# Moving the low-half subtraction of gathered token blocks to GpSimd, with x kept multiplied by 8

## The chip, the cores and the metric

One Trainium2 chip, of which the kernel uses one core. The metric is device time in microseconds (us) of one execution. The engines are named as in the profile: PE is TensorE (PEld its weight loads), DVE is VectorE, ACT is ScalarE, POOL is GpSimd, SP is SyncE, which here only issues DMAs. All engines run their own instructions in order, and wait for each other by semaphores.

## The reference

Two stages. First an attention over q, k, v of shape (8, 8, 576, 64): the sum of a coarse attention (tokens averaged in fours, its result repeated four times) and a local one (each token attends to those less than 4 away). Its output, laid out as x of 4608 tokens by 512, goes into a mixture of 8 experts with a fixed capacity of 576 tokens each:

```
logits = x @ w_gate                       # (4608, 8)
order = np.argsort(-logits.flatten())     # best (token, expert) pair first
for idx in order:                         # a token goes to the first expert that still has room
    tok, e = idx // E, idx % E
    if assigned[tok] >= 0 or counts[e] >= cap: continue
    assigned[tok] = e; counts[e] += 1
for e in range(E):
    mask = assigned == e
    out[mask] = np.maximum(x[mask] @ w1[e], 0) @ w2[e]     # 512 -> 1024 -> 512
```

## The kernel before

The first 280 us of the profile are the attention (class Attention). It works through 36 blocks of 128 tokens. For each block `norm` (L399) divides the local result by its softmax sum, `log_a` adds the coarse result, `store` writes the block of x to DRAM (x_dram), and `log_t` and `log_m` compute the gate's logits: x is transposed on PE, scaled by XS = 32 into a float16 high half and a float16 low half (L498, L499), and multiplied by the gate weights. The coarse result is normalized by the same `norm`, called in `down_v`. The order of this stage is written out by hand and does not depend on the engines' times.

Then the experts. The greedy assignment is solved one expert at a time: `Routing.phase` finds which expert fills next, and at what threshold, by counting. Compares on DVE (L709), counting matmuls on PE (L743, L750, L757, in PSUM tiles pR) and small DVE steps (L747, L752, L759, L729, L735) alternate in a long chain; at its end a one-hot product on PE (L992) and `idx` on DVE (L1001) give the 576 token numbers. Each phase needs the one before it. Below, E0 to E7 are the experts in the order in which they are found and run, and the phase of a later expert runs beside the matrix work of an earlier one.

For one expert:

- `weights` loads w1 and w2 (4 loads of 1 MB, from SP's queue, L1032); `split` turns each into a float16 high half on ACT (wh, L1048) and low half on DVE (wl, L1050).
- `gather` fetches the tokens in five blocks c = 0 to 4 (four of 128 tokens, one of 64) by indirect DMA issued on GpSimd (xg, L1065). `piece_dma(c)` then makes the high half of the block, scaled by XM = 8, on ACT (xs, L1084), the low half on DVE (L1085), and has SP transpose both by DMA into xt (L1086). There are XSB = 2 buffers xs, so the third block waits until the first transpose is done. Only E0 uses `piece` instead, which transposes on PE (L1074 to L1078).
- `mlp` computes the first product in eight passes f (pH, L1101; in each pass the first 256 tokens, then the other 320, with three matmuls for high by high, high by low and low by high), with ht split into halves on ACT and DVE (L1114, L1117); then the second product in five blocks c (pX, L1130, 24 matmuls each, 120 in all, in two PSUM buffers), which ACT scales into y (L1135) and GpSimd scatters to the output by indirect DMA (out_dram, L1138).

The order here is not written by hand: a scheduler that estimates the instructions' times lists them per engine. `in2` places the gathered blocks of the next expert: blocks 0 and 1 are to be issued after y of block c = 0, blocks 2 and 3 after c = 1, block 4 after c = 2 (table GET; for E1 this is a lower bound only, since its gather comes later). The subtraction and the copy are marked as high priority. A DVE instruction that waits therefore holds every DVE instruction behind it, those of the routing too, and PE's counting matmuls stand in PE's queue between those of pH and pX, so that PE waits with them.

Of the kernel before, what the change touches and what calls it, by code (L numbers as in the profile page):

```python
# [11 lines left out]
AF = mybir.ActivationFunctionType  # L12
OP = mybir.AluOpType
# [16 lines left out]
NTOK = B * S  # L30
NT = NTOK // 128
E, F = 8, 1024
XS = 32.0
GSN = ('k2',)
SH1 = 0.416
EARLY = 1
# [53 lines left out]
class Attention:  # L90
# [273 lines left out]
    def down_v(self, b, g):  # L364
        nc = self.nc
        vd = self.vd[b % 2]
        pt = self.ptd[b]
        o = self.ps.tile([128, 512], F32, name="g", bufs=8)

        nc.tensor.matmul(o[:, :260], pt[:, 9], vd[:, 1, 4 * g:4 * g + 4].rearrange("p h d -> p (h d)"),  # L370
                         start=True, stop=False, skip_group_check=True)
        for j in range(4):
            nc.tensor.matmul(o[:, 65 * j:65 * j + 65], pt[:, 4 * g + j], vd[:, 0, 4 * g + j],  # L373
                             start=False, stop=True, skip_group_check=True)
        x = self.wk.tile([128, 5, D], F32, name="xu", bufs=2)
        if g:

            for i in range(2):
                for c in range(2):
                    for hp in range(HP):  # L380
                        r = slice(32 * hp, 32 * hp + 32)
                        nc.tensor.matmul(o[r, 260 + 65 * i:325 + 65 * i], pt[:, 10 if c else 8, r], vd[:, c, 2 * hp + i],
                                         start=c == 0, stop=c == 1, skip_group_check=True, tile_position=(0, 32 * hp))
        def end():
            r = self.norm(o, x[:, :4], 4 + g, 4.0)
            up = self.up_dram[b * G:b * G + 128, 256 * g:256 * g + 256]
            nc.sync.dma_start(up, x[:, :4].rearrange("p h d -> p (h d)"))
            if g:
                own = self.wk.tile([128, 2], F32, name="own")
                nc.vector.tensor_tensor(own, r[:, 4:].to_broadcast([128, 2]), self.half, op=OP.mult)  # L390
                y = x[:, 4]
                nc.vector.tensor_scalar(y, o[:, 260:324], own[:, :1], None, op0=OP.mult)
                nc.vector.scalar_tensor_tensor(y, o[:, 325:389], own[:, 1:], y, op0=OP.mult, op1=OP.add)
                nc.sync.dma_start(bass.AP(tensor=up.tensor, offset=up.offset - 256 * g + 128 * HD,
                                          ap=[[D, H], [HD, 16], [1, D]]), y)

        self.after(FN, end, ("v", b, g))

    def norm(self, o, dst, m, n):  # L399
# [67 lines left out]
    def loc_v(self, u, g):  # L467
        nc = self.nc
        if g == 0:
            self.x[u] = self.wk.tile([128, HD], F32, name="x", bufs=XB)  # L470
        x = self.x[u]
        o = self.ps.tile([128, 512], F32, name="g", bufs=8)
        pt = self.ptw[u % NPT]
        for h in range(4):
            for i in range(2):
                nc.tensor.matmul(o[64 * i:64 * i + 64, 65 * h:65 * h + 65],  # L476
                                 pt[:, 2 * g + i, h].rearrange("p b q -> p (b q)"),
                                 self.vw[u % 4][:, i, 4 * g + h], start=True, stop=True)
        self.norm(o, x[:, 256 * g:256 * g + 256].rearrange("p (h d) -> p h d", h=4), 4, 1.0)

    def log_a(self, u):
        nc = self.nc
# [6 lines left out]
    def log_t(self, u):  # L489
# [3 lines left out]
        for c in range(4):  # L493
# [3 lines left out]
        hi = xt[:, 0].rearrange("p c t -> p (c t)")  # L497
        nc.scalar.activation(hi, pf, AF.Copy, scale=XS)  # L498
        self.after(FT, lambda: nc.vector.scalar_tensor_tensor(xt[:, 1].rearrange("p c t -> p (c t)"), pf, XS, hi,  # L499
                                                              op0=OP.mult, op1=OP.subtract), ("x", u))  # L500
# [116 lines left out]
            self.nc.tensor.matmul(p, w, w[:, None].to_broadcast([128, 4, 128]), start=True, stop=True)  # L617
# [1 line left out]

W1S, W2S, XM = 64.0, 64.0, 8.0  # L620
LOP = 512
CAP = NTOK // E
LV = ((64, 1024), (32, 32), (32, 1))
SW = 16
WHOLE = ((0, NT),)
HALF = {16: ((0, NT),), 32: ((0, 20), (20, NT)), 64: ((0, 20), (20, NT)), 128: ((0, 12), (12, 24), (24, NT))}
XSB = 2
LOE = "vector"
RACT = True
EH = ((0, 18), (18, NT))  # L630
SPP = ("xh", "xl")
# [373 lines left out]
class Experts:  # L1005
# [50 lines left out]
    def gather(self, idx, first):  # L1056


        nc = self.nc
        xt = self.wk.tile([128, 2, 4, CAP], F16, name="xt")  # L1060
        xgs = []
        for c, (s0, n) in enumerate(SL):
            xg = self.wk.tile([128, HD], F32, name="xg", bufs=5)
            with self.tc.high_priority():
                self.fetched = nc.gpsimd.indirect_dma_start(out=xg[:n], out_offset=None, in_=self.x,  # L1065
                                                            in_offset=bass.IndirectOffsetOnAxis(
                                                                ap=idx[:n, c:c + 1], axis=0))
            xgs.append(xg)

        def piece(c):  # L1070
            s0, n = SL[c]
            p = self.ps.tile([128, 4, 128], F32, name="pX", bufs=2)
            for d in range(4):
                nc.tensor.transpose(p[:, d, :n], xgs[c][:n, 128 * d:128 * d + 128], self.ident[:n, :n])  # L1074
            hi, lo = xt[:, 0, :, s0:s0 + n], xt[:, 1, :, s0:s0 + n]
            with self.tc.high_priority():
                nc.scalar.activation(hi, p[:, :, :n], AF.Copy, scale=XM)
                nc.vector.scalar_tensor_tensor(lo, p[:, :, :n], XM, hi, op0=OP.mult, op1=OP.subtract)  # L1078

        def piece_dma(c):  # L1080
            s0, n = SL[c]
            xs = self.wk.tile([128, 2, HD], F16, name="xs", bufs=XSB)
            with self.tc.high_priority():
                nc.scalar.activation(xs[:n, 0], xgs[c][:n], AF.Copy, scale=XM)  # L1084
                getattr(nc, LOE).scalar_tensor_tensor(xs[:n, 1], xgs[c][:n], XM, xs[:n, 0], op0=OP.mult, op1=OP.subtract)  # L1085
                nc.sync.dma_start_transpose(xt[:, :, :, s0:s0 + n].rearrange("p a d s -> p (a d) s"),  # L1086
                                            xs[:n].rearrange("p a d -> p (a d)"))

        return xt, piece if first else piece_dma
# [182 lines left out]
```

## Time and profile before

| | us |
|---|---|
| median of 3 runs | 774.69 (771.76 to 777.55) |
| profiled execution | 782.95 |
| its span | 781.0 |
| PE busy | 677.3 (87%) |
| DVE busy | 539.3 (69%) |
| ACT busy | 334.7 (43%) |
| POOL busy | 243.7 (31%) |
| mean granted PE clock | 0.935 of full speed |

Starts of the experts' first product on the profile's time axis (first pH matmul): E0 326.97, E1 392.50, E2 453.87, E3 516.74, E4 579.94, E5 629.60, E6 676.65, E7 723.71 us. From E5 on an expert takes 47 us; E0 to E3, beside which the routing runs, take 61 to 66.

How to read the rows: "L743" is line 743 of the kernel. A row of a timeline gives start, duration, engine, line, operation, output<-inputs, shapes, and in brackets how long the engine had been idle and what released it. A row of waits gives who waited for whom, the total, the count and the longest. A row that begins with two times joined by a colon is a window: its length, and busy time and count of each engine in it.

### The profile page before, as it was taken

Reading aid. Unit: us, or ns where it says so; the run is one execution under the profiler, and the core shown is the slowest. Engines: PE = TensorE matmul, PEld = TensorE weight load, DVE = VectorE, ACT = ScalarE, POOL = GpSimd, SP = SyncE. Lnnn points to the kernel's source line nnn. Section 1 sums busy time; section 2 is a strip of 40 time slices with the busy share of each in tenths; the row PEclk is TensorE's granted clock in tenths of the full one; section 3 lists DMA queues with packets and bytes.
Section 4 is the critical chain, followed back from the end, with each engine's and each line's share of the span. In section 5 each row is a group of like instructions: output and inputs, shape, how many; then the busy total and the mean of one; then the engine's idle time right before and its main releaser. Section 6 shows DMA issues by size and latency. Waiting matters only on the chain.

```text
span 781.0 us, 21139 instructions
## 1 busy us (share of the span) xinstructions
PE 677.3 (87%) x8545; PEld 469.2 (60%) x8545; DVE 539.3 (69%) x1614; ACT 334.7 (43%) x646; POOL 243.7 (31%) x280
## 2 busy tenths in 40 slices
PE   6888997998998953399699899879899999999994
PEld 3677786786877742265375366347357476574752
DVE  6977887987878886588779698849879245271210
ACT  3428676485675531343326144315225344352210
POOL 8263564535627430600512212220220311301001
PEclk9779999999999975599999999979999999999998
DMA  9977889998999742513726662863663832604001
GB/s 282 195 205 190 228 208 256 224 261 237 216 264 233 182 142 60 175 44 130 227 52 234 133 237 61 203 195 138 178 160 142 230 113 85 152 1 102 21 28 34
DMA packets 152900, 126.17 MB, mean 162 GB/s; under 512 B 96996, under 2 KB 127204, under 8 KB 152804
## 3 DMA queue, kind: packets, MB, share of 16 engines
q1 hardware_dynamic: 145424, 103.30, 50.1%
q0 software_dynamic: 6432, 20.98, 8.8%
q8 instruction: 68, 1.11, 0.6%
q10 hardware_dynamic: 948, 0.55, 0.3%
q14 instruction: 28, 0.23, 0.1%
HBM read 95.30 MB, written 21.23 MB: 149 GB/s over the span
## 4 chain that ended last, share of the span: by engine, by line
issue 29%; PE 25%; DVE 23%; DMA 12%; POOL 4%; ACT 4%; SPq 1%; another core or an unknown queue 0%; POOLq 0%; ACTq 0%; DVEq 0%
PE pX L1130 5%; PE pH L1101 4%; DMA xt<-xs 3%; POOL out_dram L1138 3%; DVE cmp L709 2%; PE g L292 2%; PE g L476 2%; DMA nat<-in_k_dram 2%; DMA up_dram<-xu 2%; PE pR L743 2%; DMA nat<-in_q_dram 2%; DMA xg<-x_dram,idx 2%; DVE wl L1050 1%; PE g L373 1%; DVE kt L276 1%
## 5 line engine op out<-in xcount | busy, mean ns | idle before, releaser
L1101 PE MATMUL pH<-xt,wh 128*128 128x256 f16 (+1 forms) x1024 | 196.1, 289 | 2.2 <-DVE ht L1117 1.5
L1130 PE MATMUL pX<-wh,ht 128*128 128x512 f16 (+1 forms) x640 | 183.3, 386 | 0.0
L1101 PE MATMUL pH<-xt,wl 128*128 128x320 f16 (+1 forms) x512 | 147.4, 289 | 0.0
L1138 POOL DMA_INDIRECT out_dram<-y,idx x40 | 45.0, 1124 | 294.7 <-ACT y L1135 272.7
L1130 PEld LDWEIGHTS <-ht 128*128 128x128 f16 (+1 forms) x960 | 81.2, 101 | 91.6 <-issue 8.2
L1130 PE MATMUL pX<-wl,ht 128*128 128x512 f16 (+1 forms) x320 | 119.9, 386 | 0.0
L1101 PEld LDWEIGHTS <-wh 128*128 128x128 f16 x1024 | 98.9, 99 | 31.5 <-issue 5.0
L1114 ACT ACTIVATE ht<-pH 128x512 f16<-128x512 f32 (+1 forms) x128 | 45.4, 407 | 106.9 <-PE pH L1101 102.8
L1050 DVE SCALAR_TENSOR_TENSOR wl<-nat,wh 128x512 f16<-128x512 f32 x128 | 84.9, 684 | 2.7
L1065 POOL DMA_INDIRECT xg<-x_dram,idx x40 | 46.8, 1170 | 98.5 <-DVE idx L1001 40.2
L1117 DVE SCALAR_TENSOR_TENSOR ht<-pH,ht 128x512 f16<-128x512 f32 (+1 forms) x128 | 52.4, 449 | 36.0 <-ACT ht L1114 35.8
L1135 ACT ACTIVATE y<-pX 128x512 f32<-128x512 f32 (+1 forms) x40 | 23.8, 594 | 119.2 <-PE pX L1130 86.8
L1048 ACT ACTIVATE wh<-nat 128x1024 f16<-128x1024 f32 x64 | 66.8, 1056 | 4.1 <-DMA nat<-in_moe_w_dram 3.9
L1085 DVE SCALAR_TENSOR_TENSOR xs<-xg,xs 128x512 f16<-128x512 f32 (+1 forms) x35 | 23.7, 688 | 51.3 <-ACT xs L1084 45.1
L1101 PEld LDWEIGHTS <-wl 128*128 128x128 f16 x512 | 50.5, 99 | 12.7
L465 ACT COPY pt<-g 64x512 f32<-64x512 f32 x72 | 41.7, 579 | 38.1 <-PE g L454 36.8
L292 PE MATMUL g<-ident,nat 128*128 128x128 f32 x256 | 39.9, 290 | 9.0 <-DMA nat<-in_k_dram 4.4
L476 PE MATMUL g<-vw,pt 128*64 128x65 f32 x1152 | 44.2, 227 | 3.3 <-ACT pt L465 1.9
L476 PEld LDWEIGHTS g<-vw,pt 128*64 128x64 f32 x1152 | 39.2, 140 | 10.4 <-ACT pt L465 6.2
L278 ACT COPY kt<-g 64x512 f32<-64x512 f32 (+1 forms) x53 | 33.4, 631 | 22.5 <-PE g L292 11.1
L265 POOL TENSOR_TENSOR gtmp<-qz 64x576 f32<-64x576 f32 x28 | 32.3, 1154 | 31.9 <-DVE kdt L268 24.1
L499 DVE SCALAR_TENSOR_TENSOR xt<-g,xt 128x512 f16<-128x512 f32 x36 | 24.6, 684 | 22.1 <-ACT xt L498 22.0
(220 smaller groups left out, 1167.2 us busy)
## 6 DMA issues: line engine op xcount, KB each, us to landing
nat<-in_moe_w_dram SPq DMA_DIRECT2D x28, 1024.0 KB
vw<-in_v_dram SPq DMA_DIRECT2D x136, 96.0 KB
up<-up_dram SPq DMA_DIRECT2D x36, 256.0 KB
x_dram<-x SPq DMA_DIRECT2D x36, 256.0 KB
nat<-in_q_dram SPq DMA_DIRECT2D x16, 512.0 KB
nat<-in_k_dram SPq DMA_DIRECT2D x16, 512.0 KB
nat<-in_v_dram SPq DMA_DIRECT2D x14, 512.0 KB
up_dram<-xu SPq DMA_DIRECT2D x16, 128.0 KB
```

Of the source, the lines that this page charges most:

```text
L278: self.nc.scalar.copy(out, in_)
L292: nc.tensor.transpose(p[:, a, :, fp], src[:, 4 * hh + 2 * a + s, 2 * fp:2 * fp + 2].rearrange("p f d -> p (f d)"), self.ident)
L465: self.nc.scalar.copy(out, in_)
L476: nc.tensor.matmul(o[64 * i:64 * i + 64, 65 * h:65 * h + 65], pt[:, 2 * g + i, h].rearrange("p b q -> p (b q)"), self.vw[u % 4][:, i, 4 * ...
L1048: nc.scalar.activation(hi, r, AF.Copy, scale=sc)
L1050: nc.vector.scalar_tensor_tensor(lo[:, a:a + LOP], r[:, a:a + LOP], sc, hi[:, a:a + LOP], op0=OP.mult, op1=OP.subtract)
L1065: self.fetched = nc.gpsimd.indirect_dma_start(out=xg[:n], out_offset=None, in_=self.x, in_offset=bass.IndirectOffsetOnAxis(ap=idx[:n, c:c ...
L1101: mm = nc.tensor.matmul(p[:, s, :s1 - s0], w[d][a][:, 128 * f:128 * f + 128], xt[:, b, d, s0:s1], start=j == 0, stop=j == len(seq) - 1)
L1114: last = nc.scalar.activation(hi, q, AF.Relu)
L1117: nc.vector.scalar_tensor_tensor(lo, q, 0.0, hi, op0=OP.max, op1=OP.subtract)
L1130: nc.tensor.matmul(p[o:o + m], ht[:, f, h0:h0 + m], w[4 + f // 2][b][:, 512 * (f % 2):512 * (f % 2) + 512], start=j < parts, stop=j >= len ...
L1138: i = nc.gpsimd.indirect_dma_start(out=self.out, in_=y[:n], in_offset=None, out_offset=bass.IndirectOffsetOnAxis(ap=idx[:n, c:c + 1], axis=0))
```

## The change

x is multiplied by 8 where it is normalized: both calls of `norm` divide by a denominator that is 8 times smaller, so x, x_dram and the coarse result hold 8 times the value, and the gate's scale XS becomes 4. The gathered blocks then need no scale: the high half is a plain copy to float16, and the low half a plain subtraction, in `piece` (E0) as in `piece_dma` (E1 to E7). In `piece_dma` this subtraction is issued on GpSimd instead of VectorE (LOE), and there are five buffers xs instead of two (XSB), one for each block of an expert. The diff adds one line near the top, so that from line 33 on every line number of the changed kernel is one higher than before. The scheduler then orders the instructions of the expert stage anew.

```diff
--- before.py
+++ after.py
@@ -30,7 +30,8 @@
 NTOK = B * S
 NT = NTOK // 128
 E, F = 8, 1024
-XS = 32.0
+XM = 8.0
+XS = 32.0 / XM
 GSN = ('k2',)
 SH1 = 0.416
 EARLY = 1
@@ -382,7 +383,7 @@
                         nc.tensor.matmul(o[r, 260 + 65 * i:325 + 65 * i], pt[:, 10 if c else 8, r], vd[:, c, 2 * hp + i],
                                          start=c == 0, stop=c == 1, skip_group_check=True, tile_position=(0, 32 * hp))
         def end():
-            r = self.norm(o, x[:, :4], 4 + g, 4.0)
+            r = self.norm(o, x[:, :4], 4 + g, 4.0 / XM)
             up = self.up_dram[b * G:b * G + 128, 256 * g:256 * g + 256]
             nc.sync.dma_start(up, x[:, :4].rearrange("p h d -> p (h d)"))
             if g:
@@ -476,7 +477,7 @@
                 nc.tensor.matmul(o[64 * i:64 * i + 64, 65 * h:65 * h + 65],
                                  pt[:, 2 * g + i, h].rearrange("p b q -> p (b q)"),
                                  self.vw[u % 4][:, i, 4 * g + h], start=True, stop=True)
-        self.norm(o, x[:, 256 * g:256 * g + 256].rearrange("p (h d) -> p h d", h=4), 4, 1.0)
+        self.norm(o, x[:, 256 * g:256 * g + 256].rearrange("p (h d) -> p h d", h=4), 4, 1.0 / XM)
 
     def log_a(self, u):
         nc = self.nc
@@ -617,15 +618,15 @@
             self.nc.tensor.matmul(p, w, w[:, None].to_broadcast([128, 4, 128]), start=True, stop=True)
 from contextlib import nullcontext
 
-W1S, W2S, XM = 64.0, 64.0, 8.0
+W1S, W2S = 64.0, 64.0
 LOP = 512
 CAP = NTOK // E
 LV = ((64, 1024), (32, 32), (32, 1))
 SW = 16
 WHOLE = ((0, NT),)
 HALF = {16: ((0, NT),), 32: ((0, 20), (20, NT)), 64: ((0, 20), (20, NT)), 128: ((0, 12), (12, 24), (24, NT))}
-XSB = 2
-LOE = "vector"
+XSB = 5
+LOE = "gpsimd"
 RACT = True
 EH = ((0, 18), (18, NT))
 SPP = ("xh", "xl")
@@ -1074,15 +1075,15 @@
                 nc.tensor.transpose(p[:, d, :n], xgs[c][:n, 128 * d:128 * d + 128], self.ident[:n, :n])
             hi, lo = xt[:, 0, :, s0:s0 + n], xt[:, 1, :, s0:s0 + n]
             with self.tc.high_priority():
-                nc.scalar.activation(hi, p[:, :, :n], AF.Copy, scale=XM)
-                nc.vector.scalar_tensor_tensor(lo, p[:, :, :n], XM, hi, op0=OP.mult, op1=OP.subtract)
+                nc.scalar.copy(hi, p[:, :, :n])
+                nc.vector.tensor_tensor(lo, p[:, :, :n], hi, op=OP.subtract)
 
         def piece_dma(c):
             s0, n = SL[c]
             xs = self.wk.tile([128, 2, HD], F16, name="xs", bufs=XSB)
             with self.tc.high_priority():
-                nc.scalar.activation(xs[:n, 0], xgs[c][:n], AF.Copy, scale=XM)
-                getattr(nc, LOE).scalar_tensor_tensor(xs[:n, 1], xgs[c][:n], XM, xs[:n, 0], op0=OP.mult, op1=OP.subtract)
+                nc.scalar.copy(xs[:n, 0], xgs[c][:n])
+                getattr(nc, LOE).tensor_tensor(xs[:n, 1], xgs[c][:n], xs[:n, 0], op=OP.subtract)
                 nc.sync.dma_start_transpose(xt[:, :, :, s0:s0 + n].rearrange("p a d s -> p (a d) s"),
                                             xs[:n].rearrange("p a d -> p (a d)"))
 
```

## The prediction

> **What bounds the kernel now.** I read the page first, then windows, then TensorE's own timeline. E0 to E7 are the experts in the order in which they run; L1101 is the first product (pH), L1130 the second (pX), L743 to L992 the routing of a later expert. The page (VectorE's busy tenths and TensorE's clock in 40 slices), and two windows of the last third (columns: window, length, PE busy, PEld, DVE, ACT, POOL, PE clock, DMA share, GB/s):
>
> ```profile
> span 781.0 us, 21139 instructions
> PE 677.3 (87%) x8545; PEld 469.2 (60%) x8545; DVE 539.3 (69%) x1614; ACT 334.7 (43%) x646; POOL 243.7 (31%) x280
> DVE  6977887987878886588779698849879245271210
> PEclk9779999999999975599999999979999999999998
> 620.00:660.00 40.00, 40.00 (x281) 26.15 (x279) 19.28 (x36) 17.74 (x32) 6.29 (x7) 1.00 0.35 103
> 660.00:700.00 40.00, 40.00 (x280) 26.03 (x279) 18.13 (x34) 16.05 (x29) 9.24 (x10) 1.00 0.40 90
> ```
>
> From 620 us on TensorE never stops: nothing can be won there. Before that it stops, and its timeline names for whom (in brackets the idle time ahead and its releaser):
>
> ```profile
> 382.65 0.39 PE L743 MATMUL pR<-oh,cmp 128*128 128x32 bf16 x9 [2.70 <-DVE cmp L709]
> 390.50 0.39 PE L743 MATMUL pR<-oh,cmp 128*128 128x32 bf16 x9 [2.46 <-DVE cmp L709]
> 439.28 0.17 PE L757 MATMUL pR<-fl,head 128*128 128x8 bf16 x1 [2.37 <-DVE fl L752]
> 508.99 0.90 PE L992 MATMUL pR<-r,ohl 128*128 128x72 bf16 x12 [4.03 <-DVE ohl L988]
> 522.22 0.25 PE L750 MATMUL pR<-cs,id 128*128 128x8 f16 x4 [2.46 <-DVE cs L747]
> 566.81 0.39 PE L743 MATMUL pR<-oh,cmp 128*128 128x32 bf16 x9 [2.42 <-DVE cmp L709]
> ```
>
> What VectorE did just before (its timeline at those places), and its and ScalarE's waits after 330 us (total, times, longest):
>
> ```profile
> 381.24 0.69 DVE L1085 SCALAR_TENSOR_TENSOR xs<-xg,xs 128x512 f16<-128x512 f32 x1 [2.71 <-ACT xs L1084]
> 389.08 0.69 DVE L1085 SCALAR_TENSOR_TENSOR xs<-xg,xs 128x512 f16<-128x512 f32 x1 [0.89 <-ACT xs L1084]
> 391.99 0.69 DVE L1085 SCALAR_TENSOR_TENSOR xs<-xg,xs 64x512 f16<-64x512 f32 x1
> 438.46 0.69 DVE L1085 SCALAR_TENSOR_TENSOR xs<-xg,xs 128x512 f16<-128x512 f32 x1 [1.95 <-ACT xs L1084]
> 504.71 0.68 DVE L1085 SCALAR_TENSOR_TENSOR xs<-xg,xs 64x512 f16<-64x512 f32 x1 [2.42 <-ACT xs L1084]
> 521.97 0.19 DVE L747 TENSOR_SCALAR cs<-pR 128x32 f16<-128x32 f32 x1 [2.50 <-remote]
> 564.97 0.69 DVE L1085 SCALAR_TENSOR_TENSOR xs<-xg,xs 128x512 f16<-128x512 f32 x1 [1.89 <-ACT xs L1084]
> DVE xs L1085 <- ACT xs L1084: 45.1, 18, 5.1
> ACT xs L1084 <- DMA xt<-xs: 23.0, 15, 3.3
> ```
>
> Five of the six stops are one thing: VectorE stands at the low half of a gathered block, with a routing step that TensorE needs queued behind it. The subtraction waits for ScalarE's high half, which waits for one of two xs buffers until a transpose has left it. The sixth (522.22) has no xs ahead: VectorE idled 2.50 us for something outside the queues. Three stops are followed by a slow clock (column before the last two):
>
> ```profile
> 390.00:400.00 10.00, 9.50 (x97) 6.45 (x98) 7.72 (x24) 3.29 (x7) 2.56 (x2) 0.83 0.38 81
> 440.00:450.00 10.00, 10.00 (x84) 4.65 (x82) 5.35 (x23) 1.28 (x3) 1.41 (x1) 0.83 0.31 67
> 500.00:510.00 10.00, 5.97 (x45) 3.07 (x44) 7.13 (x14) 2.02 (x4) 3.47 (x2) 0.91 1.02 290
> 510.00:520.00 10.00, 9.19 (x86) 4.48 (x83) 4.64 (x19) 0.59 (x1) 5.08 (x6) 0.75 0.92 304
> ```
>
> **The change, part by part.** The scaling by 8 moves into constants of instructions that are there anyway (the factor in L404, the scale of L498 and L499); it is a power of two, so the routing sees the same numbers. Shapes and counts stay, and in the attention the order on every engine stays. A scaled copy becomes a plain one on ScalarE (L1084, L1077) and a scaled subtraction a plain one: nothing; were the copy 0.1 us longer, its 40 instructions lie on an engine that is idle 57% of the span. What moves is the order after E0. VectorE while E1's blocks are prepared, before:
>
> ```order
> L735 SCALAR_TENSOR_TENSOR rest<-nj,tabs 128x33
> L1050 SCALAR_TENSOR_TENSOR wl_6592<-nat,wh_6591 128x512
> L1085 SCALAR_TENSOR_TENSOR xs<-xg,xs 128x512
> L709 TENSOR_TENSOR cmp_6771<-xh,thr_6769 128x1152
> L1085 SCALAR_TENSOR_TENSOR xs<-xg,xs 128x512
> L747 TENSOR_SCALAR cs<-pR 128x32
> ```
>
> and of the change (every line number is one higher):
>
> ```order
> L736 SCALAR_TENSOR_TENSOR rest<-nj,tabs 128x33
> L1051 SCALAR_TENSOR_TENSOR wl_6592<-nat,wh_6591 128x512
> L710 TENSOR_TENSOR cmp_6771<-xh,thr_6769 128x1152
> L1051 SCALAR_TENSOR_TENSOR wl_6592<-nat,wh_6591 128x512
> L748 TENSOR_SCALAR cs<-pR 128x32
> ```
>
> The compare no longer stands behind a block that has yet to arrive. GpSimd's queue from the gather of E3 on, during E2's second product, before:
>
> ```order
> L1065 DMA xg<-x_dram,idx 128x512 x4
> L1065 DMA xg<-x_dram,idx 64x512
> L1138 DMA out_dram<-y,idx 4608x512 x4
> L1065 DMA xg<-x_dram,idx 128x512 x4
> L1065 DMA xg<-x_dram,idx 64x512
> ```
>
> and now:
>
> ```order
> L1066 DMA xg<-x_dram,idx 128x512 x4
> L1066 DMA xg<-x_dram,idx 64x512
> L1139 DMA out_dram<-y,idx 4608x512
> L1086 TENSOR_TENSOR xs<-xg,xs 128x512 x2
> L1139 DMA out_dram<-y,idx 4608x512
> L1086 TENSOR_TENSOR xs<-xg,xs 128x512 x2
> L1066 DMA xg<-x_dram,idx 128x512 x4
> L1139 DMA out_dram<-y,idx 4608x512
> L1086 TENSOR_TENSOR xs<-xg,xs 64x512
> ```
>
> The subtractions came in between scatters, and E3's last one stands behind four gathers of E4, which wait for E4's indices. Those come earlier too: their matmul (L992) follows 49 of E2's 120 pX matmuls instead of 96.
>
> GpSimd's prices (ns min/median/max; the first GpSimd row is the first gather of the run), and two neighbours on VectorE that subtract or add as many elements:
>
> ```profile
> L248 POOL TENSOR_TENSOR vd<-gtv,identb x8: 1042/1043/1139, 21.6 to 255.1; 128x512 f32<-128x512 f32 x8
> L241 POOL TENSOR_TENSOR gtv<-nat x16: 1263/1273/1610, 16.0 to 252.0; 128x512 f32<-128x512 f32 x16
> 314.78 6.47 POOL L1065 DMA_INDIRECT xg<-x_dram,idx  x1 [27.93 <-DVE used L956]
> L1065 POOL DMA_INDIRECT xg<-x_dram,idx x35: 906/966/1486, 375.8 to 674.3; - x35
> 381.36 1.35 POOL L1065 DMA_INDIRECT xg<-x_dram,idx  x1 [0.30 <-issue]
> L1085 DVE SCALAR_TENSOR_TENSOR xs<-xg,xs x35: 677/691/693, 381.2 to 717.1; 128x512 f16<-128x512 f32 x28, 64x512 f16<-64x512 f32 x7
> L484 DVE TENSOR_TENSOR x<-x,up x27: 680/775/1145, 62.4 to 250.2; 128x512 f32<-128x512 f32 x27
> ```
>
> A GpSimd subtraction with f16 output is in no row; its bounds are 1.04 us (L248) and 1.61 (L241's longest). I take 1.27, L241's median: like L241, and unlike L248, it reads two full tensors. So 35 x 0.69 = 24 us leave VectorE, 35 x 1.27 = 44 us come to GpSimd. Now each stop:
>
> (a) E0 to E1, 2.70 + 2.46: E1's blocks become the next late thing. GpSimd is in gathers until 381.36 + 1.35 = 382.71; five subtractions (6.35), one scatter (taken at a gather's median, 0.97) and about 1.0 of gaps (0.3 ahead of a DMA, as in the gather's row) make 8.3, so the last low half stands at 391.0 against 391.99 + 0.69 = 392.68 now. At most 1.7 of the 5.16 is won; the fourth block's transpose starts no earlier than now, so I take 0.5, and count no gain in clock, since a stop of that length stays.
> (b) 439.28: 2.37, and clock (1 - 0.83) x 10 = 1.7. High and low halves no longer wait for a transpose, by the order E2's indices come 15 pH matmuls earlier, and ScalarE still converts the last block after the third of pX's five parts, so it is ready before pX ends: 4.1.
> (c) 508.99: 4.03, and clock 0.9 + 2.5 = 3.4, of which some 0.4 falls into the idle time: 7.0. Whether E3's last block, behind E4's gathers, is in time follows from four more rows:
>
> ```profile
> 513.40 0.98 POOL L1065 DMA_INDIRECT xg<-x_dram,idx  x1 [6.13 <-DVE thr L729]
> 386.07 0.63 ACT L1084 ACTIVATE xs<-xg 128x512 f16<-128x512 f32 x1 [1.97 <-DMA xt<-xs]
> 653.12 0.38 PE L1130 MATMUL pX<-wh,ht 128*128 128x512 f16 x1
> 676.65 0.39 PE L1101 MATMUL pH<-xt,wh 128*128 128x256 f16 x2
> ```
>
> From L992 (508.99) to the gather (513.40) it takes 4.4; four gathers 4 x 1.27 = 5.1; scatter and subtraction 2.5; a transpose some 4.1 (from 381.93, the low half's end, to 386.07, when its buffer is free): 16.1. TensorE has 71 of 120 pX matmuls left, 71/120 x (676.65 - 653.12) = 13.9, the first half pass of pH, 12 matmuls, 1.3, and six small groups of routing matmuls, about 3: 18. It is in time by 2 us, an estimate that can be off by that much.
> (d) 566.81: 2.42, no slow clock: 2.4.
>
> Together 14.0. Against it: (e) In the late transitions TensorE has no gaps, so the blocks must not be late:
>
> ```profile
> 659.43 0.97 POOL L1138 DMA_INDIRECT out_dram<-y,idx  x1 [27.21 <-ACT y L1135]
> 673.36 0.68 DVE L1085 SCALAR_TENSOR_TENSOR xs<-xg,xs 64x512 f16<-64x512 f32 x1 [4.52 <-ACT xs L1084]
> ```
>
> From 659.43 GpSimd now runs three scatters and four gathers (7 x 0.97 + 7 x 0.3) and five subtractions (6.35): the last low half at 674.7, against 674.04. That is 0.7 later, where pH starts at 676.65 with the first two blocks and wants this one from about 678. Two such transitions: 0.6, between 0 and 1.4.
> (f) GpSimd and VectorE slow each other: L484, which ran while GpSimd added, took 0.10 (median) to 0.47 us (maximum) more than its own 0.68 minimum, while L1085 without GpSimd arithmetic beside it never left 0.69. Twenty subtractions fall where VectorE matters: 2 to 9 us of its time, of which TensorE sees little. I take 1, of 0 to 5. The Trainium skill (SBUF — State Buffer, Who interferes with whom) says that a VectorE instruction with two SBUF inputs and a GpSimd instruction that reads SBUF block each other for a whole instruction. The trace agrees in kind and shows less than a whole one; in full it is the rival "lock".
> (g) The routing stands earlier and closer: 1 for more short waits, of 0 to 7.
>
> Sum: -14.0 + 2.6 = -11.4. The profiled execution took 782.95 us (span 781.0), 1.1% more than the median of 774.69; so 771.55, or by the ratio 0.9854 x 774.69 = **763.4 us**.
>
> **The rivals.**
> - *More*: the 2.46 us stop at 522.22 and its slow clock (1.7) fall elsewhere or away, and short waits shrink as VectorE has 24 us less to do: about 5 more, 758. For it: its cause is no xs. Against: such a wait can return at any place. 0.20.
> - *Lock*: every subtraction holds VectorE for its whole 1.27 us: 20 x 1.27 = 25.4 against 20 x 0.69 = 13.8 removed, 11.6 on VectorE, all handed to TensorE: about 0, 774. Against: L484's median. 0.10.
> - *Order*: the routing is packed so that TensorE waits for VectorE often: (g) at 7, -5.4, 769. For it: the page's slices 18 to 30 (340 to 590 us) have VectorE busy 8 or 9 tenths in most. 0.12.
> - *GpSimd's queue turns slow*: no row shows arithmetic on GpSimd after a gather, and the first gather took 6.47 against 0.97. If each turn between the two cost 5.5, five turns in each of seven transitions would make blocks 27 us late: 7 x 25 = +175, about 940. It decides early: 0.5 us a turn makes a block 2.5 us late, seven times 17 with the slow clock, and the change is slower. The Trainium skill (GPSIMD Engine Reference, 2.1 Instruction dispatch) has about 6 us for the first call of a freshly loaded GpSimd kernel, with no instruction of its own in a profile; by that rule 6.47 is paid once and nothing here. The trace, with all later gathers at 0.9 to 1.5, agrees. 0.08.
>
> **How the numbers follow.** The forecast has 0.50. A measurement of this kernel tells about 1%, 7.7 us, from no change. Of the forecast 0.47, of *more* 0.20 and of *order* and *lock* 0.04 lie below 767: faster 0.71. Same: 0.03 + 0.16 = 0.19 (*order* mostly, *lock*, which may also slip past 1%: 0.02). Slower: 0.08 + 0.02 = 0.10. The range leaves out *slow* and the far half of *lock*, and below a part of *more*: 754 to 773.
>
> **What would show it.** Right: no L1085-like row on DVE, TensorE's stops before L743, L757 and L992 under 1 us, granted clock 1.00 around 440 and 510, and a stop of some 5 us before the first pH of E1, named xt or GpSimd xs. GpSimd's subtraction at 1.27. Wrong: stops before pH in the late transitions (queue), L1050 or L709 longer than now (lock), many stops of about 1 us before routing matmuls (order), or a gather over 2 us behind a subtraction.

## The result and the profile after

The change made the kernel slower: a median of 783.48 us (776.79 to 785.80, 12 runs) against 775.62 us (771.76 to 779.09, 12 runs), a ratio of 1.0095 with a 95% interval of 1.0066 to 1.0124. The forecast was 763.4 us, a gain of 1.5%.

The page of the changed kernel (busy times of the engines, VectorE's busy tenths and TensorE's clock in 40 slices), and the two windows of the last third:

```profile
span 784.1 us, 21156 instructions
PE 676.5 (86%) x8545; PEld 468.7 (60%) x8545; DVE 535.5 (68%) x1579; ACT 332.9 (42%) x646; POOL 284.8 (36%) x315
DVE  5977887779787886588879899859876144170210
PEclk8979999899999985599999999999999999999998
620.00:660.00 40.00, 40.00 (x281) 26.21 (x280) 17.61 (x33) 16.97 (x31) 11.16 (x11) 1.00 0.49 130
660.00:700.00 40.00, 40.00 (x270) 25.04 (x269) 12.77 (x25) 15.46 (x28) 15.37 (x15) 1.00 0.40 89
```

35 subtractions of 0.69 us, 24 us, left VectorE, but its busy time fell by only 3.8 us (539.3 to 535.5): 20 us came back. The last third is as full as before, so the late blocks are in time. TensorE's timeline shows these stops (idle time ahead of a row, in brackets) of more than 1.4 us between 380 and 580 us:

```profile
386.83 0.17 PE L758 MATMUL pR<-fl,head 128*128 128x8 bf16 x1 [4.11 <-DVE fl L753]
391.90 0.39 PE L744 MATMUL pR<-oh,cmp 128*128 128x32 bf16 x9 [1.95 <-DVE cmp L710]
438.11 0.17 PE L758 MATMUL pR<-fl,head 128*128 128x8 bf16 x1 [2.01 <-DVE fl L753]
445.57 0.39 PE L744 MATMUL pR<-ol,cmp 128*128 128x32 bf16 x9 [1.85 <-DVE cmp L710]
453.25 0.19 PE L782 MATMUL pR<-one,f 128*72 128x1 bf16 x1 [1.51 <-DVE f L933]
500.55 0.74 PE L993 MATMUL pR<-r,ohl 128*128 128x72 bf16 x18 [1.56 <-DVE r L984]
506.37 0.65 PE L744 MATMUL pR<-oh,cmp 128*128 128x16 bf16 x18 [3.99 <-DVE oh L859]
570.69 0.22 PE L782 MATMUL pR<-one,f 128*72 128x1 bf16 x1 [2.76 <-DVE f L933]
```

They stand at the same transitions as before and again name VectorE, though no subtraction stands in its queue any more. What VectorE did at six of these places, from its timeline (start, duration):

```profile
384.37 2.33 DVE L1051 SCALAR_TENSOR_TENSOR wl<-nat,wh 128x512 f16<-128x512 f32 x1 [3.05 <-ACT wh L1049]
387.49 3.56 DVE L730 SCALAR_TENSOR_TENSOR thr<-nj,rest 128x32 int16<-128x32 f32 x1
434.87 3.11 DVE L1051 SCALAR_TENSOR_TENSOR wl<-nat,wh 128x512 f16<-128x512 f32 x1
442.67 2.04 DVE L730 SCALAR_TENSOR_TENSOR thr<-nj,tabs 128x32 int16<-128x32 f32 x1
502.86 2.54 DVE L953 TENSOR_TENSOR asg<-asg,n 128x36 f32<-128x36 f32 x1
567.28 3.02 DVE L932 SCALAR_TENSOR_TENSOR f<-amu,code,gg 128x36 bf16<-128x36 bf16 x1
```

and GpSimd beside it (the row at 497.53 has no partner above):

```profile
383.87 2.27 POOL L1086 TENSOR_TENSOR xs<-xg,xs 128x512 f16<-128x512 f32 x2
387.62 3.37 POOL L1086 TENSOR_TENSOR xs<-xg,xs 128x512 f16<-128x512 f32 x3
435.15 2.27 POOL L1086 TENSOR_TENSOR xs<-xg,xs 128x512 f16<-128x512 f32 x2
442.39 2.27 POOL L1086 TENSOR_TENSOR xs<-xg,xs 128x512 f16<-128x512 f32 x2
497.53 3.99 POOL L1086 TENSOR_TENSOR xs<-xg,xs 128x512 f16<-128x512 f32 x2
503.07 2.26 POOL L1086 TENSOR_TENSOR xs<-xg,xs 128x512 f16<-128x512 f32 x2
567.98 2.26 POOL L1086 TENSOR_TENSOR xs<-xg,xs 128x512 f16<-128x512 f32 x2
```

Each VectorE row ends 0.1 to 0.6 us behind a row of two or three back-to-back subtractions: 384.37 + 2.33 = 386.70 against 383.87 + 2.27 = 386.14; 387.49 + 3.56 = 391.05 against 390.99; 567.28 + 3.02 = 570.30 against 570.24. L730, a [128, 32] step of 0.18 us, took 3.56. From 300 us on, ten VectorE rows are over 0.35 us longer than is usual for their line and shape, 18.8 us together (18.6 in a second trace); before has none in three traces. The time over the usual one is called the excess below. At 497.53 it goes the other way: two subtractions take 3.99 us instead of 2.27, while VectorE runs L989 and L980. That a row of one engine ends only when the other's is through I call the *hold*.

One number compares the traces best: the expert stage, from the first pH matmul of E0 to the end of TensorE's last matmul. The time ahead of it differs between executions of one kernel by up to 6 us (the routing's last GpSimd memset starts at 286.71, 280.56 and 284.42 us in the three traces of before), the stage by 0.6 to 2.4 us: 443.9, 442.6, 445.0 before; 445.4, 444.8 after.

### The profile page after: what moved, and what is told of

It is laid out like the page before. It is cut to its first block, busy times and chain, and to the rows that moved or that the text cites. A ratio compares the mean times of both kernels' runs of the same rounds, so it can differ in the third digit from the quotient of the medians.

```text
span 784.1 us, 21156 instructions
## 1 busy us (share of the span) xinstructions
PE 676.5 (86%) x8545; PEld 468.7 (60%) x8545; DVE 535.5 (68%) x1579; ACT 332.9 (42%) x646; POOL 284.8 (36%) x315
## 4 chain that ended last, share of the span: by engine, by line
PE 49%; DVE 25%; issue 9%; ACT 6%; DMA 5%; POOL 3%; SPq 1%; POOLq 0%; ACTq 0%; DVEq 0%
PE pX L1131 15%; PE pH L1102 14%; DVE cmp L710 3%; PE g L477 3%; DVE wl L1051 3%; PE g L293 2%; PE pR L744 2%; DVE ht L1118 2%; PE g L437 2%; PE g L326 2%; PE g L455 2%; PE g L374 2%; ACT pt L466 1%; DMA vw<-in_v_dram 1%; ACT qz L279 1%
## 5 line engine op out<-in xcount | busy, mean ns | idle before, releaser
L1102 PE MATMUL pH<-xt,wh 128*128 128x256 f16 (+1 forms) x1024 | 192.8, 286 | 2.9 <-DVE ht L1118 2.2
L1131 PE MATMUL pX<-wh,ht 128*128 128x512 f16 (+1 forms) x640 | 185.4, 390 | 0.0
L1139 POOL DMA_INDIRECT out_dram<-y,idx x40 | 45.1, 1127 | 281.9 <-ACT y L1136 252.7
L1051 DVE SCALAR_TENSOR_TENSOR wl<-nat,wh 128x512 f16<-128x512 f32 x128 | 88.7, 715 | 6.2 <-ACT wh L1049 3.0
L1066 POOL DMA_INDIRECT xg<-x_dram,idx x40 | 46.5, 1163 | 70.8 <-DVE used L957 27.9
L1138 DVE SCALAR_TENSOR_TENSOR y<-pX,y 64x512 f32<-64x512 f32 x8 | 5.5, 693 | 88.8 <-ACT y L1136 88.7
L266 POOL TENSOR_TENSOR gtmp<-qz 64x576 f32<-64x576 f32 x28 | 32.0, 1141 | 35.0 <-DVE kdt L269 27.2
L1086 POOL TENSOR_TENSOR xs<-xg,xs 128x512 f16<-128x512 f32 (+1 forms) x35 | 41.6, 1210 | 0.5
```

The costliest lines, as they stand in the source:

```text
L1051: nc.vector.scalar_tensor_tensor(lo[:, a:a + LOP], r[:, a:a + LOP], sc, hi[:, a:a + LOP], op0=OP.mult, op1=OP.subtract)
L1086: getattr(nc, LOE).tensor_tensor(xs[:n, 1], xgs[c][:n], xs[:n, 0], op=OP.subtract)
L1102: mm = nc.tensor.matmul(p[:, s, :s1 - s0], w[d][a][:, 128 * f:128 * f + 128], xt[:, b, d, s0:s1], start=j == 0, stop=j == len(seq) - 1)
L1131: nc.tensor.matmul(p[o:o + m], ht[:, f, h0:h0 + m], w[4 + f // 2][b][:, 512 * (f % 2):512 * (f % 2) + 512], start=j < parts, stop=j >= len ...
L1139: i = nc.gpsimd.indirect_dma_start(out=self.out, in_=y[:n], in_offset=None, out_offset=bass.IndirectOffsetOnAxis(ap=idx[:n, c:c + 1], axis=0))
```

## The experiments

The theory: the hold costs the change what its buffers win. The rivals: the new, denser order of the routing costs it; the late transitions do; or the loss lies in the attention, with the scale.

Each is compared with before as it ran in the same session, since the median of before moves from session to session (medians 778.23 for e1 to e4, 780.16 for e5 to e7, 774.09 for e9 to e11, 779.46 for e12 and e13).

| run | median us | ratio to before, 95% interval | expert stage us | long VectorE rows, their excess us |
|---|---|---|---|---|
| change | 783.48 | 1.0095, 1.0066 to 1.0124 | 445.4 | 10, 18.8 |
| e1 before, plus GpSimd subtractions | 800.19 | 1.0297, 1.0218 to 1.0375 | 465.1 | 15, 29.7 |
| e2 change, GpSimd only writes | 762.13 | 0.9795, 0.9701 to 0.9889 | 429.0 | 4, 4.3 |
| e3 change, one GpSimd input | 775.58 | 0.9955, 0.9916 to 0.9994 | 440.1 | 14, 8.0 |
| e4 change, VectorE subtracts | 769.85 | 0.9897, 0.9823 to 0.9971 | 433.1 | 0 |
| e5 GpSimd for E1 to E4 | 784.52 | 1.0055, 1.0008 to 1.0103 | 448.0 | 9, 17.6 |
| e6 GpSimd for E5 to E7 | 766.72 | 0.9810, 0.9725 to 0.9894 | 431.7 | 0 |
| e7 e4, memset into xg | 772.41 | 0.9895, 0.9806 to 0.9984 | 428.2 | 0 |
| e9 e6, separate memset | 758.38 | 0.9792, 0.9741 to 0.9844 | 427.4 | 0 |
| e10 before, separate memset | 764.88 | 0.9864, 0.9808 to 0.9919 | 435.2 | 0 |
| e11 change again | 781.18 | 1.0096, 1.0050 to 1.0142 | 444.8 | 10, 18.6 |
| e12 scale alone | 779.64 | 1.0033, 0.9994 to 1.0072 | 444.0 | 0 |
| e13 five buffers alone | 765.67 | 0.9837, 0.9779 to 0.9895 | 431.7 | 0 |

**e1: the suspected cost added to before.**

```diff
 nc.vector.scalar_tensor_tensor(xs[:n, 1], xgs[c][:n], XM, xs[:n, 0], op0=OP.mult, op1=OP.subtract)
+nc.gpsimd.tensor_tensor(junk[:n], xgs[c][:n], xs[:n, 0], op=OP.subtract)   # junk: [128, 512] f16, 5 buffers (shortened)
```

> The kernel before, and behind each VectorE low half of a gathered block one GpSimd subtraction of the same operands into a tile that nobody reads: nothing of the output changes, and the order on TensorE, VectorE, ScalarE and SyncE is word for word that of before; GpSimd's queue alone has 35 instructions more. Theory 'hold' (a GpSimd subtraction keeps VectorE from starting or ending an instruction with two SBUF inputs until a whole row of back-to-back subtractions is over; in the trace of the change twelve VectorE instructions are 0.8 to 3.4 us too long, 19 us together): 8 to 20 us slower than before, 784 to 795, with stretched VectorE rows beside every pair of the added subtractions. Rival 'order' (the denser routing order of the change costs the time, the hold is hidden): within 2 us of before. Rival 'queue' (gathers stand later in GpSimd's queue): slower, but with no VectorE row longer than before.

22 us slower, more than the 8 to 20 expected, at an order that differs only in GpSimd's queue. Rows of VectorE, and of GpSimd, in its timelines:

```profile
433.21 2.64 DVE L729 SCALAR_TENSOR_TENSOR thr<-nj,rest 128x32 int16<-128x32 f32 x1
437.82 3.10 DVE L1050 SCALAR_TENSOR_TENSOR wl<-nat,wh 128x512 f16<-128x512 f32 x1
```

```profile
433.52 2.27 POOL L1085 TENSOR_TENSOR junk<-xg,xs 128x512 f16<-128x512 f32 x2
438.10 2.27 POOL L1085 TENSOR_TENSOR junk<-xg,xs 128x512 f16<-128x512 f32 x2
```

They end together again (435.85 and 435.79; 440.92 and 440.37). The expert stage is 21 us longer and the long rows' excess is 29.7 us, of which 6.7 us (three rows) lie behind 620 us, where TensorE does not wait: with the routing in VectorE's queue, TensorE pays most of what VectorE loses. 'Order' (within 2 us) falls. 'Queue' asked for no long VectorE row; there are 15. That the later gathers cost a part of the 21 us beside the hold is not excluded by this run.

**e2 and e3: the change, with less read.**

```diff
-nc.gpsimd.tensor_tensor(xs[:n, 1], xgs[c][:n], xs[:n, 0], op=OP.subtract)
+nc.gpsimd.memset(xs[:n, 1], 0.0)                                            # e2
+nc.gpsimd.tensor_scalar(xs[:n, 1], xgs[c][:n], 0.0, None, op0=OP.mult)      # e3
```

> The changed kernel with the GpSimd subtraction replaced by a GpSimd memset of the same low half, which reads no SBUF (the low halves are left out of the result, as zeros). The order on TensorE, VectorE and ScalarE is word for word that of the change; GpSimd's row can start before its block has arrived. 'Hold': no VectorE row is stretched, and the time falls by the 14 us that the prediction had hoped for or more: 762 to 770. 'Order': 783 as the change, give or take 2.

> The changed kernel with the GpSimd subtraction replaced by a GpSimd multiplication of the block alone by 0 (one SBUF input instead of two; the low halves are left out of the result, as zeros). The order on TensorE, VectorE and ScalarE is that of the change. 'Hold' by any reading instruction, for as long as it lasts: between e2 and the change, by its duration against 1.16 us; VectorE rows stretched beside it. If only a second input makes it hold: as e2. 'Order': 783.

In e2 the rows of three memsets pass beside VectorE without a trace; its timeline and GpSimd's at E1's blocks:

```profile
372.47 0.19 DVE L730 SCALAR_TENSOR_TENSOR thr<-nj,rest 128x32 int16<-128x32 f32 x1
372.69 0.76 DVE L710 TENSOR_TENSOR cmp<-xh,thr 128x1152 bf16<-128x1152 int16 x1
```

```profile
372.57 1.47 POOL L1086 MEMSET xs<- 128x512 f16 x3
```

The stage is 16 us shorter than the change's at the same order on TensorE, VectorE and ScalarE. The memset is also shorter (0.54 against 1.16 us) and waits for less, so the 16 us are an upper bound for what the hold costs there. The median gained another 5 us ahead of the stage, for a reason of its own (e9). Three of the four long rows left are one chain at 541 us (L973 and what stands behind it), beside a gather and a memset.

From e3, GpSimd's timeline and VectorE's:

```profile
381.75 5.88 POOL L1086 TENSOR_SCALAR xs<-xg 128x512 f16<-128x512 f32 x4
384.53 0.83 DVE L730 SCALAR_TENSOR_TENSOR thr<-nj,rest 128x32 int16<-128x32 f32 x1
```

In e3 GpSimd's instruction is longer than the subtraction (median 1.51 us), but the longest excess of a VectorE row is 0.85 us and the sum 8.0: beside a row with one input VectorE's steps came through before the row was over, beside rows with two they mostly did not. The loss shrinks with the hold: the stage is 5 us shorter than the change's. But it is still 7 us longer than e4's, which has no hold: either the price of the hold is not in proportion to its excess, or the longer instruction costs something else. No run tells these apart. My "by its duration against 1.16 us" was wrong: longer, it holds less.

**e4, e12, e13: the parts alone.** e4 is the change with `LOE = "vector"`; e13 is before with `XSB = 5`; e12 is before with the scale moved into the attention and plain copies and subtractions.

> The changed kernel with the subtraction back on VectorE: five xs buffers, x kept times 8, plain copies. 'Hold': no VectorE row stretched; the high halves no longer wait for transposes, so the low halves no longer block VectorE for 3 to 5 us: 765 to 773, faster than before. 'Order' (five buffers bring the dense order): 780 to 785. If neither the buffers nor the scale matter: 774 to 777.

> The other part alone: five xs buffers, x not scaled, the scaled subtraction on VectorE as before. By e4, which had the same order on TensorE, GpSimd and SyncE and gained 1%: from the first product of E0 to the end about 433 us instead of 443, 768 to 771. If e4's gain came from the scale and the plain forms: as before.

> One part alone: x kept times 8 from its normalization on, plain copies and plain subtractions, but two xs buffers and the subtraction on VectorE. The order on every engine is that of before. From the first product of E0 to the end the change loses 1.8 us against before in two traces each, its median 7 to 8. If the rest of that comes with the scale (in the attention): 779 to 782 where before takes 775, 0.5 to 0.9% slower. If the scale is free, as the prediction had it: within 2 us of before, and the rest of the loss stays unplaced.

Five buffers alone, with the new order that they bring, are worth 1.6% (stage 431.7, 12 us less; the median is below the 768 to 771 expected). The row of the waits "ACT xs L1084 <- DMA xt<-xs", 23.0 us in before, is gone; TensorE's timeline from 370 us on has these stops over 1 us left:

```profile
375.60 0.39 PE L743 MATMUL pR<-oh,cmp 128*128 128x32 bf16 x9 [2.54 <-DVE cmp L709]
422.24 0.24 PE L750 MATMUL pR<-cs,id 128*128 128x8 f16 x4 [1.03 <-DVE cs L747]
503.22 0.39 PE L743 MATMUL pR<-oh,cmp 128*128 128x32 bf16 x9 [1.52 <-issue]
505.15 0.25 PE L750 MATMUL pR<-cs,id 128*128 128x8 f16 x4 [1.11 <-DVE cs L747]
```

VectorE still does all 35 subtractions and still waits at them, 38.3 us in 15 waits, down from 45.1 in 18. Most of that lies in the last third, where TensorE does not wait. Between 330 and 580 us the same row fell from 12.6 us to 5.0 (all of e13, then that window in before and in e13):

```profile
DVE xs L1085 <- ACT xs L1084: 38.3, 15, 3.9
DVE xs L1085 <- ACT xs L1084: 12.6, 9, 2.7
DVE xs L1085 <- ACT xs L1084: 5.0, 6, 2.5
```

With the scale added (e4) the stage is 433.1. From there, moving the subtraction to GpSimd (the change) costs 12 us and gives all of it back. Added up from the traces, TensorE is idle in the stage for 27.9 us in both traces of the change, all of it named VectorE, against 18.0 in e4, 17.0 in e13 and 22.8 to 25.3 in before. So 10 of the 12 us are idle time, and VectorE is what TensorE waits for. The order of e4 is not that of the change, but e2, which has the change's order on TensorE, VectorE and ScalarE, is 4 us shorter than e4, so the order does not explain the loss. Nor do late blocks: no stop of the change names xt. The scale alone is 2.6 us slower by its ratio, whose interval includes no difference; its stage is that of before.

**e5 and e6: where it costs.**

```diff
-getattr(nc, LOE).tensor_tensor(
+(nc.gpsimd if ng <= 4 else nc.vector).tensor_tensor(     # e5; e6: ng > 4; ng: number of the expert
```

> The change with the subtraction on GpSimd for the blocks of E1 to E4 alone, and on VectorE for E5 to E7, where VectorE is idle most of the time and TensorE never stops. 'Hold' costs only where VectorE's next routing step is waited for, which is before about 600 us: as the change, 781 to 785. If the late transitions carry the loss: as e4, about 770.

> The other half: GpSimd subtracts the blocks of E5 to E7, VectorE those of E1 to E4. 'Hold' that costs only early: as e4 (five buffers, all on VectorE), 768 to 772. If the late transitions carry the loss: about 783.

Both came out as 'hold' had them: GpSimd for E1 to E4 has the change's long rows and its stage, GpSimd for E5 to E7 has none and is 1.9% faster than before. In the late transitions VectorE has little to do (4 tenths or less in eight of the last nine slices of the page), and TensorE waits for none of it. e6's median is below the 768 to 772 expected. Between e6 and e13 no difference is shown.

**e7, e9, e10: the first gather.** In e2 the first gather took 1.19 us; its twin in the other kernels 6.47. In e2 a memset stood ahead of it.

```diff
+if first and c == 0: nc.gpsimd.memset(xg[:, :1], 0.0)                                    # e7, on e4
+if first and c == 0: nc.gpsimd.memset(self.wk.tile([128, 1], F16, name="warm", bufs=1), 0.0)   # e9 on e6, e10 on before
```

> e4 (five buffers, subtraction on VectorE) with a GpSimd memset of one column of the first gathered tile ahead of the first gather. In e2, where a GpSimd memset stood at that place by chance, the first gather took 1.19 us, in all other kernels 6.47. If the memset is what shortens it: the first product starts 5 us earlier after the routing, 764 to 766, the first gather at 1.2. If the 6.47 is a price of the first gather itself (code that has to be loaded once): 6.47 again and as e4, 770.

> e6 (VectorE subtracts the blocks of E1 to E4, GpSimd those of E5 to E7, five buffers) with one GpSimd memset of a [128, 1] tile ahead of the first gather; the order on every engine is that of e6 but for this instruction. If the memset takes over the waits on earlier buffers and the first gather's start-up then runs behind its wait for the indices: the first gather at 1.2 instead of 6.47 us, the first product of E0 some 5.8 us earlier after the routing's last memset (34.4 instead of 40.3, as in e2), about 761. If e2's short gather had another cause: 766 to 767.

> The kernel before with the same memset alone, order otherwise word for word that of before. First gather at 1.2 us and the time 5 to 6 us under before; if the memset does nothing, as before.

GpSimd's timeline in e10 (the row of before stands in the prediction: 314.78, 6.47, ended by "used L956"):

```profile
285.12 0.11 POOL L1065 MEMSET warm<- 128x1 f16 x1
312.56 1.19 POOL L1066 DMA_INDIRECT xg<-x_dram,idx  x1 [27.33 <-DVE idx L1001]
```

The memset takes over the gather's waits for the buffers' earlier users. In before an instruction that only waits, for 27.2 us, stands right ahead of the gather; in e10 there is none, and the gather waits by itself. It then starts with the indices and is short: from the routing's last memset to E0's first product it takes 34.5 us instead of 40.2. In e7 the gather was as short, but the memset wrote the gather's own tile, so the scheduler put that block's gather behind the weight loads and E0 started 5 us later (45.3): the gain was lost, and the 764 to 766 expected were missed. e9 has the lowest median, 758.38 us, but its ratio (0.9792) is no different from e6's (0.9810); only the traces show the memset's gain there, 34.4 us instead of 40.3 from the routing's last memset to E0's first product. In e10 the stage was 8 us shorter too, more than was expected, at the same order. The stop that before has at 522.22, of 2.39 to 2.46 us in its three traces, is missing there, and TensorE is busy for 415.2 us of the stage instead of 418.5 to 422.1; why is not settled (one trace).

**e8, e11, e14: how far the traces repeat.**

> The kernel before once more, for a second trace of it: the attention until the routing's last GpSimd memset took 286.7 us in the first trace, 280 to 288 in the others of nearly the same attention, so the two traces are compared from that point on. From there to the end: 494 us in the first trace; if the change costs 8 us there, this one shows 485 to 490; if the change costs it in the attention, 494 again.

> The changed kernel once more, for a second trace: from the first product of E0 to the end it took 445.4 us in the first trace, before 443.9 and 442.6, and e5, which differs only after 580 us, 448.0. If the hold costs what the medians say (8 us), this one shows 446 to 451; if the loss lies in the attention, 443 to 445 and a first product later than 325.

> A third trace of before: from the first product of E0 to the end 442.6 to 443.9 if that stage repeats itself as in the first two, and the attention again between 280 and 288.

The stage repeats: 442.6 to 445.0 in before, 444.8 and 445.4 in the change, with the same stops to 0.1 us in e11 (4.10, 1.89, 2.01, 1.84, 1.51, 1.56, 4.00, 2.75). From the routing's last memset to the end of the span, e8 took 492.9 us against 494.3 in the first trace, near the second of its two cases. e14's stage, 445.0, is above the 443.9 expected. e11 fits neither of its cases: 444.8 speaks against a cost of 8 us in the stage, and its first product, at 322.71, is not later than 325.

## Why the prediction was wrong

**Bound and stops.** Right: the six stops, and that two xs buffers made VectorE stand at the low halves ahead of steps that TensorE needs (12.6 us before 580 us, 5.0 with five buffers). e13 shows the worth of it, 12 us in the stage against the 14.0 of (a) to (d), though it leaves the subtraction on VectorE. What I had put down to both edits belongs to the buffers.

**Step (f), "GpSimd and VectorE slow each other ... I take 1, of 0 to 5", failed.** It was sized from L484 in the attention, whose rows were 0.10 (median) to 0.47 us longer than the shortest. I did not ask whether those rows lay beside GpSimd instructions for their full length (9 of the 27 overlap no GpSimd addition at all), nor what a row of several would do. Measured: 18.8 us of VectorE time, in holds of up to 3.4 us, and 12 us of the stage (change against e4). With 12 in place of 1, the sum is -11.4 + 11 = about 0, near the 1.3 us by which the stages differ (445.1 against 443.8, means of two and three traces). The misjudged term thus accounts for 11 of the 19 us between the forecast change (-11.4) and the measured one (+7.9); most of the rest is the open part below.

The Trainium skill (SBUF — State Buffer, Who interferes with whom) was the better guide: a VectorE instruction with two SBUF inputs and a GpSimd instruction that reads SBUF exclude each other, and a GpSimd instruction that only writes does not. The traces agree: subtraction 18.8 us, memset none on two-input rows like those shown for e2. They go beyond it in that the hold lasted for a whole row of subtractions (3.37 us for three), and fall short of it with one GpSimd input (e3).

**The rivals.** *Lock* named the mechanism and got 0.10. Its price, 20 x 1.27 against 20 x 0.69, "about 0, 774", was the right size for the stage; I set its chance by L484's median, a row from another place. Its sign, L1050 longer than now, came: 3.11 us instead of 0.68. *Order* falls: e2 has the dense order and the shortest stage of e1 to e6. *GpSimd's queue* falls: gathers behind a subtraction take 0.9 to 1.6 us. *More* falls with the forecast, though the stop at 522.22 did go.

**Stop by stop.** (a) E1's blocks were not late: no stop named xt, and the 5 us forecast before E1's first pH did not come; 4.11 and 1.95 us stand before L758 and L744, from the hold. (b) and (d) remain as 2.01 + 1.85 and 2.76. (c) remains as 1.56 + 3.99, behind held rows again (L984 and, at 502.86, L953 with 2.54 us). The clock is 1.00 from 440 to 450 us as forecast, at that transition in both traces of the change and in e13 (0.78 to 0.89 in the three of before), but still low around 510 (column before the last two):

```profile
440.00:450.00 10.00, 8.15 (x82) 3.92 (x80) 6.24 (x21) 2.59 (x5) 3.36 (x4) 1.00 0.38 84
500.00:510.00 10.00, 5.45 (x52) 2.67 (x52) 7.96 (x19) 0.44 (x1) 7.09 (x7) 0.79 0.85 212
510.00:520.00 10.00, 9.05 (x81) 4.23 (x80) 4.59 (x21) 1.26 (x3) 4.97 (x5) 0.87 0.64 180
```

 (e) cost nothing. The price of a subtraction was 1.16 us against the 1.27 taken.

**Open.** By the medians the change loses 7.9 us, and 7.1 in e11; the stages show 1.3. The rest lies ahead of E0's first product or in executions that left no trace. Whether the scale edit has a part in it, e12 does not tell (-0.5 to 5.6 us). The traces show none: the routing's last memset starts at 284.3 us in the mean of the ten with the scale (279.90 to 288.40) and at 283.1 in the six without (279.93 to 286.71).

## What to carry to other kernels

Before work goes from VectorE to GpSimd, look at what VectorE does at that moment: while GpSimd worked through a row of two-input instructions here, VectorE's steps with two inputs in SBUF mostly stood still, however small, and a short chain that another engine waits for then waits for the whole row. Such work goes where VectorE is idle (E5 to E7 here), not where it is busy. When a change has two parts, cost each alone: here the buffer count was worth 1.6%, and the move to the other engine took it back.

## What was not expected of the hardware

- The hold covers a whole row of back-to-back GpSimd subtractions: a 0.18 us step took 3.56 us beside three of them. It works both ways: two subtractions took 3.99 us instead of 2.27 beside VectorE's L989 and L980. Steps that read one of their tensors from PSUM were not held: L763 (pR) took its usual 0.23 us beside the row of two at 561.40.
- A GpSimd instruction with one input, though longer (1.51 us), held VectorE for 0.85 us at most; beside memsets two-input steps kept their time, except behind L973 and L939, steps with a single tensor input.
- VectorE instructions with a single tensor input were caught as well, L920 for 1.76 us instead of 0.22 and, in e1, L834 for 2.65 instead of 0.17.
- The first gather took 6.45 to 6.47 us in the twelve traces in which a separate wait stands in front of it and 1.19 in the four in which it waits by itself. The Trainium skill (GPSIMD Engine Reference, 2.1 Instruction dispatch) has about 6 us for the first call of a freshly loaded GpSimd kernel. The 5.3 us of difference fit a load that runs behind the gather's own wait; no run here shows the load itself.
